# A fused convolution and feed-forward kernel: array halves by token stream, two-bank evictions, quarter-array convolution, a new prologue

## The chip, the core and the metric

The kernel runs on one core of a Trainium2 chip. The core has TensorE (PE, with its weight loads PEld), VectorE (DVE), ScalarE (ACT), GpSimd (POOL) and SyncE (SP), each with its own queue of instructions that it works through in order, and 16 DMA engines that serve transfers issued from those queues. The metric is the device time of one execution in microseconds (us), as the median of several runs. A profiled execution gives, besides its own time, a span: from the first to the last instruction of the program.

## The reference

Input x has 8 sequences of 3904 tokens, 192 features each: 31232 tokens. A causal convolution with 7 taps comes first; the 192 features are 8 heads of 24, and each head has its own softmaxed taps. Then two products with a multiplication between them.

```python
w = softmax(weight)                        # 8 heads x 7 taps
out[b, s, head] = sum_k w[head, k] * x_pad[b, s + k, head]   # 6 zeros ahead of each sequence
x = out.reshape(B * S, D)                  # 31232 x 192
a = x @ w1                                 # 192 -> 1024
b = x @ w2                                 # 192 -> 1024
h = a * b @ w3                             # 1024 -> 1024
return h @ w_out                           # 1024 -> 192
```

Both kernels use that (a * b) @ w3 @ w_out = (a * b) @ (w3 @ w_out): the 1024 x 192 product W is made once on the chip.

## The kernel before

**Convolution.** Tokens go in 32 blocks of 976: 8 windows of 122 tokens, each window loaded with its 6 tokens of history as 128 partitions (`load_x`, L78). POOL casts a block to bf16 (`cast_x`, L185). One head is one matmul with a banded 128x122 matrix `Aband` over 8 windows x 24 features = 192 columns (L199); two heads share a PSUM tile and ACT evicts it to `convo` (L203). POOL then copies feature groups so that a token's row has 384 entries, with every group of 64 features on both sides of a 128-wide piece (L207 to L210).

**Transposing.** For blocks 0 and 1 the layout change is done on PE (`transp`, L228 to L236). From block 2 on, the rows are stored to DRAM (L214) and three DMA transposes per block, more where the ring wraps, write `xT0`, `xT1`, `xT2` (L254), rings of 4096 tokens with features on partitions.

**First product.** `first_product(c)` handles a chunk of 512 tokens. For each of 8 groups of 128 hidden features, a needs three matmuls of 64 rows and so does b: a uses partitions 0 to 63 of the array and b 64 to 127, so a pair runs side by side (L290). `pa` and `pb` are one PSUM bank each out of eight. ACT copies `pa` to bf16 `asb` (L295) and DVE multiplies it by `pb` into `abT` (L296).

**Second product.** `second_product(c, half)` makes 256 tokens x 192 outputs from 16 matmuls with the tokens as weights (L309), ACT copies them out (L312) and SP stores a chunk (L314).

**W.** w3 is loaded in 8 pieces of 128 rows, cast (half on POOL, half on ACT, L327), transposed on PE (L333), evicted by DVE (L336) and multiplied by w_out (L342). This stands after the first products of chunks 0, 1 and 2.

**Order.** The order is written out by hand: the program order of each engine is the order of the calls. After the prologue the loop takes two chunks at a time: two first products, then convolution blocks as far as needed, in between the second products of the chunks three behind. SP issues loads of x, row stores, DMA transposes and output stores in program order and waits where one of them isn't ready. POOL clears the 6 history rows of a window that begins a sequence after the block's load has landed (L83).

Of the kernel before, what the change touches and what calls it, by code (L numbers as in the profile page):

```python
# [17 lines left out]
def kernel(  # L18
# [19 lines left out]
    ST = 122  # L38
    NW = 8
    BLK = ST * NW  # L40
    NB = B * S // BLK
    BPS = S // BLK
    CH = 512
    NCH = B * S // CH
    RING = 8 * CH
    LAG = 3
    PAIR = 2
# [4 lines left out]
    psum = ctx.enter_context(tc.tile_pool(name="psum", bufs=8, space=bass.MemoryType.PSUM))  # L52
    dram = ctx.enter_context(tc.tile_pool(name="dram", bufs=3, space=bass.MemoryType.DRAM))
    ctx.enter_context(tc.manual_schedule())

    def bank(shape, dtype, name):
        return psum.tile(shape, dtype, tag="bank", name=name)

    x_rows = x.rearrange("b s d -> (b s) d")
    o_rows = out  # L60


    wsb = const.tile([128, H, K], FP32)
    nc.scalar.dma_start(out=wsb, in_=weight.partition_broadcast(128))

    def load_x(it):
        xr = work.tile([128, NW, D], FP32, tag="xr", bufs=4, name="xr")
        t0 = it * BLK
        if it == 0:
            nc.gpsimd.memset(xr[0:32, 0, :], 0.0)  # L70
            nc.sync.dma_start(out=xr[PAD:PAD + 112, 0, :], in_=x_rows[0:112, :])
            nc.sync.dma_start(out=xr[PAD + 112:128, 0, :], in_=x_rows[112:ST, :])
            nc.sync.dma_start(
                out=xr[:, 1:NW, :],
                in_=bass.AP(tensor=x.tensor, offset=(ST - PAD) * D,
                            ap=[[D, 128], [ST * D, NW - 1], [1, D]]))
        else:
            nc.sync.dma_start(  # L78
                out=xr,
                in_=bass.AP(tensor=x.tensor, offset=(t0 - PAD) * D,  # L80
                            ap=[[D, 128], [ST * D, NW], [1, D]]))
            if it % BPS == 0:
                nc.gpsimd.memset(xr[0:PAD, 0, :], 0.0)  # L83
        return xr

    xr_of = {0: load_x(0)}

    HC = DFF // 2  # L90
    wf = [stage.tile([128, DFF], FP32, tag=f"w{k}f", bufs=1, name=f"w{k}f") for k in range(3)]
    W_ROWS = ((0, 64), (64, 0), (128, 128))

    def load_w(half):
        cs = slice(half * HC, (half + 1) * HC)
        for k, (r1, r2) in enumerate(W_ROWS):
            nc.sync.dma_start(out=wf[k][0:64, cs], in_=moe_w1[r1:r1 + 64, cs])
            nc.scalar.dma_start(out=wf[k][64:128, cs], in_=moe_w2[r2:r2 + 64, cs])

    load_w(0)  # L100
    xr_of[1] = load_x(1)
    load_w(1)
    xr_of[2] = load_x(2)

    w3r = moe_w3.rearrange("(jt jp) g -> jp jt g", jp=128)
    wo_f = stage.tile([128, JT, D], FP32, tag="wof", bufs=1, name="wo_f")
    nc.sync.dma_start(out=wo_f, in_=moe_w_out.rearrange("(gt gp) d -> gp gt d", gp=128))
    w3f = []
    for jt in range(JT):
        f = stage.tile([128, DFF], FP32, tag="w3f", bufs=JT, name="w3f")  # L110
        nc.sync.dma_start(out=f, in_=w3r[:, jt, :])
        w3f.append(f)


    ident = const.tile([128, 128], BF16)
    make_identity(nc, ident)
    ones = const.tile([128, 1], BF16)
    nc.gpsimd.memset(ones, 1.0)
    dmask = const.tile([128, K, ST], BF16)
    nc.gpsimd.affine_select(  # L120
        out=dmask, in_=ones.unsqueeze(2).to_broadcast([128, K, ST]),
        pattern=[[-1, K], [-1, ST]], compare_op=ALU.is_equal,
        fill=0.0, base=0, channel_multiplier=1)
    Aband = const.tile([128, H, ST], BF16)
    nc.gpsimd.memset(Aband, 0.0)

    CW = 32 + PAD
    QC = [(0, PAD, 32), (32 - PAD, 0, CW), (64 - PAD, 0, CW), (96 - PAD, 0, ST - 96 + PAD)]
    cmask = const.tile([128, K, CW], BF16)
    nc.vector.memset(cmask, 0.0)  # L130
    for q, (c0, j0, n) in enumerate(QC):
        qs = slice(32 * q, 32 * q + 32)
        nc.vector.tensor_copy(out=cmask[qs, :, j0:j0 + n], in_=dmask[qs, :, c0:c0 + n])

    wmax = const.tile([128, H], FP32)
    nc.vector.reduce_max(out=wmax, in_=wsb, axis=AX.X)
    nc.vector.tensor_tensor(
        out=wsb, in0=wsb, in1=wmax.unsqueeze(2).to_broadcast([128, H, K]),
        op=ALU.subtract)
    nc.scalar.activation(out=wsb, in_=wsb, func=ACT.Exp)  # L140
    wsum = const.tile([128, H], FP32)
    nc.vector.reduce_sum(out=wsum, in_=wsb, axis=AX.X)
    nc.vector.reciprocal(out=wsum, in_=wsum)
    nc.vector.tensor_tensor(
        out=wsb, in0=wsb, in1=wsum.unsqueeze(2).to_broadcast([128, H, K]),
        op=ALU.mult)

    HH = H // 2
    cprod = const.tile([128, H, CW, K], FP32)
    cband = const.tile([128, H, CW], BF16)  # L150

    def bands(half):
        hs = slice(half * HH, (half + 1) * HH)
        nc.vector.tensor_tensor(
            out=cprod[:, hs].rearrange("p h j k -> p h k j"),
            in0=cmask.unsqueeze(1).to_broadcast([128, HH, K, CW]),
            in1=wsb[:, hs, :].unsqueeze(3).to_broadcast([128, HH, K, CW]),
            op=ALU.mult)
        with nc.allow_low_precision(reason="one tap and zeros"):
            nc.vector.reduce_sum(out=cband[:, hs, :], in_=cprod[:, hs], axis=AX.X)  # L160
        for q, (c0, j0, n) in enumerate(QC):
            qs = slice(32 * q, 32 * q + 32)
            dst, src = Aband[qs, hs, c0:c0 + n], cband[qs, hs, j0:j0 + n]
            if q % 2 == 0:
                nc.gpsimd.tensor_copy(out=dst, in_=src)
            else:
                nc.scalar.copy(out=dst, in_=src)  # L167


    xT0 = const.tile([128, RING], BF16)  # L170
    xT1 = const.tile([128, RING], BF16)
    xT2 = const.tile([128, RING], BF16)
    xT = (xT0, xT1, xT2)

    PE_BLOCKS = 2
    C = 2 * D

    def cast_x(it, first=False):
        xb = work.tile([128, NW, D], BF16, tag="xb", bufs=2, name="xb")
        xr = xr_of.pop(it)  # L180
        if first:
            nc.scalar.copy(out=xb[:, 0:NW // 2, :], in_=xr[:, 0:NW // 2, :])
            nc.gpsimd.tensor_copy(out=xb[:, NW // 2:NW, :], in_=xr[:, NW // 2:NW, :])  # L183
        else:
            nc.gpsimd.tensor_copy(out=xb, in_=xr)  # L185
        return xb

    convo_of = {}
    rows_of = {}
    xb_of = {}  # L190

    def conv_pair(it, t):
        if t == 0:
            convo_of[it] = work.tile([128, NW, C], BF16, tag="convo", bufs=2, name="convo")
        convo, xb = convo_of[it], xb_of[it]
        cps = bank([128, 2, NW, G], FP32, "cps")
        for r in range(2):
            h = 2 * t + r
            nc.tensor.matmul(  # L199
                cps[0:ST, r], Aband[:, h, :], xb[:, :, h * G:(h + 1) * G],  # L200
                start=True, stop=True)
        dst = convo[0:ST, :, 2 * t * G:(2 * t + 2) * G]
        nc.scalar.copy(  # L203
            out=dst.rearrange("s b (r g) -> s r b g", r=2), in_=cps[0:ST])
        if t == 3:
            del xb_of[it]
            nc.gpsimd.tensor_copy(out=convo[0:ST, :, D:D + 64], in_=convo[0:ST, :, 128:192])  # L207
            if it >= PE_BLOCKS:
                nc.gpsimd.tensor_copy(out=convo[0:ST, :, 256:320], in_=convo[0:ST, :, 64:128])  # L209
                nc.gpsimd.tensor_copy(out=convo[0:ST, :, 320:384], in_=convo[0:ST, :, 0:64])  # L210
                rows = dram.tile([NW, ST, C], BF16, tag="rows", bufs=3, name="rows")
                rows_of[it] = rows
                for a, b in ((0, 112), (112, ST)):
                    nc.sync.dma_start(out=rows[:, a:b, :].rearrange("w s c -> s w c"),  # L214
                                      in_=convo[a:b])
                del convo_of[it]

    def ring_spans(t0, n):
        a = t0 % RING
        if a + n <= RING:  # L220
            return [(0, a, n)]
        return [(0, a, RING - a), (RING - a, 0, n - (RING - a))]

    def transp(it, k):
        convo = convo_of[it]
        tps = bank([128, BLK], BF16, "tps")
        for w in range(NW):
            nc.tensor.transpose(  # L228
                out=tps[:, w * ST:(w + 1) * ST],
                in_=convo[0:ST, w, 128 * k:128 * (k + 1)],  # L230
                identity=ident[0:ST, 0:ST])
# [5 lines left out]
        if k == 1:  # L237
            del convo_of[it]


    def band_products(it):
        for t in range(4):
            conv_pair(it, t)
# [184 lines left out]
```

## Time and profile before

The median of three runs is 560.46 us (559.26 to 560.56).

| | value |
|---|---|
| profiled execution, its own time | 559.08 us |
| its span | 557.3 us |
| mean granted TensorE clock | 0.997 |
| first matmul of the first product | 19.64 us |
| first product of the loop (chunk 3) | 61.9 us |
| DMA moved | 101.60 MB, 182 GB/s mean |
| x loads, row stores, output stores | 768 B pieces |

Read it from the top: the engine shares say which engine is busy; the chain of waits says whose work ended last at each moment; the groups of instructions by line give the duration of one instruction and what its engine waited for. A matmul's recorded duration includes the pipeline, so the pace of matmuls is read from their starts, not from their durations.

### The profile page before, as it was taken

The numbers are of one execution on the slowest core, as the hardware profiler recorded it, in microseconds if no ns is written. First come the engines' busy times: TensorE is split into PE (matmuls) and PEld (weight loads), VectorE is DVE, ScalarE is ACT, GpSimd is POOL, SyncE is SP. The second block draws the span as 40 slices with busy tenths as digits, with TensorE's granted clock in tenths as the row PEclk, the third lists the DMA queues.
The fourth block names the chain that finished last, engine by engine and source line by source line (L and its number), as shares of the span: only waits on it lengthen the run. The fifth ranks groups of instructions, "written<-read, shape, count | busy, mean of one in ns | idle before, by whom it ended". The sixth has DMA issues, their size and how long they took to land.

```text
span 557.3 us, 13715 instructions
## 1 busy us (share of the span) xinstructions
PE 526.0 (94%) x5296; PEld 336.5 (60%) x5296; DVE 335.8 (60%) x516; ACT 405.9 (73%) x761; POOL 112.6 (20%) x154
## 2 busy tenths in 40 slices
PE   0868989999999999999999998999999999999997
PEld 0445666556666556666655666556666556666656
DVE  6446736765556775555776554765556775556770
ACT  2557667877777877777887777877777877776772
POOL 3445030312222112222102222212222112210000
PEclk9989999999999999999999999999999999999999
DMA  7979339997977769767788787998778893665114
GB/s 177 349 258 244 60 87 218 223 247 196 204 181 177 190 166 221 204 175 173 174 223 204 152 202 167 254 221 214 201 180 176 197 222 81 162 143 148 47 33 142
DMA packets 190321, 101.60 MB, mean 182 GB/s; under 512 B 94166, under 2 KB 188464, under 8 KB 190256
## 3 DMA queue, kind: packets, MB, share of 16 engines
q1 hardware_dynamic: 189632, 99.91, 73.3%
q10 hardware_dynamic: 624, 0.82, 0.6%
q8 instruction: 41, 0.67, 0.5%
q14 instruction: 24, 0.20, 0.1%
HBM read 31.74 MB, written 46.47 MB: 140 GB/s over the span
## 4 chain that ended last, share of the span: by engine, by line
PE 82%; issue 2%; POOL 1%; ACT 0%
PE pa L290 50%; PE ops L309 27%; PE cps L199 4%; PE pb L290 1%; POOL xb L185 1%; POOL convo L210 0%; POOL convo L209 0%; ACT osb L312 0%; POOL convo L207 0%
## 5 line engine op out<-in xcount | busy, mean ns | idle before, releaser
L296 DVE TENSOR_TENSOR abT<-asb,pb 128x512 bf16<-128x512 bf16 x488 | 317.0, 688 | 186.1 <-PE pb L290 180.5
L290 PE MATMUL pa<-xT,wb 64*128 64x512 bf16 x1464 | 325.5, 378 | 1.8 <-ACT convo L203 0.7
L290 PE MATMUL pb<-xT,wb 64*128 64x512 bf16 x1464 | 325.3, 378 | 0.6 <-DVE xT L236 0.3
L295 ACT CAST asb<-pa 128x512 bf16<-128x512 f32 x488 | 285.6, 587 | 41.6 <-PE pb L290 14.1
L290 PEld LDWEIGHTS <-wb 64*128 64x128 bf16 x2928 | 141.7, 94 | 176.8 <-issue 13.6
L309 PE MATMUL ops<-W_sb,abT 128*128 128x192 bf16 x1952 | 166.3, 246 | 0.0
L309 PEld LDWEIGHTS <-abT 128*128 128x128 bf16 x1952 | 161.3, 98 | 1.7 <-issue 1.7
L312 ACT COPY osb<-ops 128x384 f32<-128x384 f32 x122 | 58.4, 479 | 79.7 <-PE ops L309 79.2
L207 POOL COPY convo<-convo 122x512 bf16<-122x512 bf16 x32 | 19.7, 615 | 317.3 <-issue 256.9
L203 ACT CAST convo<-cps 122x384 bf16<-122x384 f32 x128 | 52.2, 501 | 6.5 <-PE cps L199 6.5
L199 PE MATMUL cps<-xb,Aband 128*122 128x192 bf16 x256 | 29.1, 258 | 22.2 <-POOL xb L183 14.7
L185 POOL CAST xb<-xr 128x1536 bf16<-128x1536 f32 x31 | 45.5, 1469 | 0.0
L199 PEld LDWEIGHTS <-Aband 128*122 128x122 bf16 x256 | 23.1, 138 | 34.1 <-issue 20.1
L210 POOL COPY convo<-convo 122x512 bf16<-122x512 bf16 x30 | 18.5, 616 | 0.0
L209 POOL COPY convo<-convo 122x512 bf16<-122x512 bf16 x30 | 18.5, 616 | 0.0
L83 POOL MEMSET xr<- 6x192 f32 x7 | 1.7, 249 | 53.6 <-DMA xr<-in_x_dram 53.6
L233 DVE COPY xT<-tps 128x976 bf16<-128x976 bf16 x4 | 2.7, 667 | 9.4 <-PE tps L228 9.3
L342 PE MATMUL wps<-wo_b,w3T 128*128 128x192 bf16 x64 | 6.6, 246 | 1.3 <-DVE w3T L336 1.1
L336 DVE COPY w3T<-w3ps 128x1024 bf16<-128x1024 bf16 x8 | 5.4, 689 | 2.9 <-PE w3ps L333 2.9
L344 ACT CAST W_sb<-wps 128x192 bf16<-128x192 f32 x8 | 2.6, 320 | 6.3 <-PE wps L342 6.3
L342 PEld LDWEIGHTS <-w3T 128*128 128x128 bf16 x64 | 5.1, 98 | 1.7 <-DVE w3T L336 1.7
L167 ACT COPY Aband<-cband 32x152 bf16<-32x152 bf16 (+1 forms) x4 | 1.2, 305 | 6.0 <-DVE cband L160 5.9
(38 smaller groups left out, 50.9 us busy)
## 6 DMA issues: line engine op xcount, KB each, us to landing
xr<-in_x_dram SPq DMA_DIRECT2D x31, 768.0 KB
out_dram<-osb SPq DMA_DIRECT2D x61, 384.0 KB
rows<-convo SPq DMA_DIRECT2D x30, 672.0 KB
w3f<-in_moe_w_dram SPq DMA_DIRECT2D x8, 512.0 KB
rows<-convo SPq DMA_DIRECT2D x30, 60.0 KB
xT<-rows SPq DMA_TRANSPOSE x111
wo_f<-in_moe_w_out_dram SPq DMA_DIRECT2D x1, 768.0 KB
xr<-in_x_dram SPq DMA_DIRECT2D x1, 672.0 KB
```

Of the source, the lines that this page charges most:

```text
L185: nc.gpsimd.tensor_copy(out=xb, in_=xr)
L199: nc.tensor.matmul(cps[0:ST, r], Aband[:, h, :], xb[:, :, h * G:(h + 1) * G], start=True, stop=True)
L203: nc.scalar.copy(out=dst.rearrange("s b (r g) -> s r b g", r=2), in_=cps[0:ST])
L207: nc.gpsimd.tensor_copy(out=convo[0:ST, :, D:D + 64], in_=convo[0:ST, :, 128:192])
L209: nc.gpsimd.tensor_copy(out=convo[0:ST, :, 256:320], in_=convo[0:ST, :, 64:128])
L210: nc.gpsimd.tensor_copy(out=convo[0:ST, :, 320:384], in_=convo[0:ST, :, 0:64])
L290: nc.tensor.matmul(dst, wb[k][rows, ft * 128:(ft + 1) * 128], xT[k][rows, r0:r0 + CH], start=(k == 0), stop=(k == 2))
L295: nc.scalar.copy(out=asb, in_=pa)
L296: nc.vector.tensor_tensor(out=ab[:, ft, :], in0=asb, in1=pb, op=ALU.mult)
L309: nc.tensor.matmul(ops[:, r, :], ab[:, jt, g * 128:(g + 1) * 128], W_sb[:, jt, :], start=(jt == 0), stop=(jt == JT - 1))
L312: nc.scalar.copy(out=osb[:, 2 * half:2 * half + 2, :], in_=ops)
L342: nc.tensor.matmul(wps, w3T[:, gt, :], wo_b[:, gt, :], start=(gt == 0), stop=(gt == JT - 1))
```

## The change

Tokens are split in two streams of 15616: the first four sequences and the last four. Partitions 0 to 63 of the array now hold 64 features of a token of stream 0 and partitions 64 to 127 the same 64 features of stream 1. A round R covers 512 tokens of each stream. `pa` is a for both streams in two PSUM banks (one tile of [128, 2, 512]), `pb` the same for b, so the eight banks are four tiles. ACT and DVE take both banks in one instruction of 1024 elements; `ops` holds 512 tokens of one stream, evicted with 768 elements.

The convolution works on windows of 58 tokens (64 partitions with history). A head is four matmuls: input rows of stream 0 or 1, output columns for the first or second half of the block's windows. Each is a 64x64 matrix. The eviction reads two banks. A token pair's row has 384 entries with no copies, so one row serves both streams; rows go to one DRAM tensor, and a round's three DMA transposes each take 512 rows. Blocks have 10, 10, 10, 26, 24 and then 32 windows of each stream. Weights are kept in two layouts, straight (`wn`) and with halves swapped (`wsw`).

In the prologue 14 matmuls on zeros come first, the Exp table is asked for early, and the convolution of blocks 1 to 3, their stores and transposes stand between the steps of the first products of rounds 0 to 2. All w3 casts are on POOL. The load of block 4 stands between the first product of round 2 and the w3 products; the second product of round 0 follows W.

```diff
-    ST = 122
-    NW = 8
-    RING = 8 * CH
-    LAG = 3
-    PAIR = 2
+    NS = 2
+    TS = B * S // NS
+    NR = -(-TS // CH)
+    RING = 4 * CH
+    LAG = 2
+    Q = 64
+    ST = Q - PAD
+    SIZES = [10, 10, 10, 26, 24] + [32] * 6
...
-    psum = ctx.enter_context(tc.tile_pool(name="psum", bufs=8, space=bass.MemoryType.PSUM))
+    psum = ctx.enter_context(tc.tile_pool(name="psum", bufs=4, space=bass.MemoryType.PSUM))
+    def banks(name):
+        return psum.tile([128, NS, CH], FP32, tag="banks", name=name)
...
+    def load_x(b):
+        for i0, n in halves_of(b):
+            xr = work.tile([128, n, D], FP32, tag="xr", bufs=2, name="xr")
...
+                    for r in range(NS):
+                        q = nc.scalar if b == 0 and r == 1 else nc.sync
+                        q.dma_start(
+                            out=xr[Q * r:Q * r + Q, w:w + m, :],
+                            in_=bass.AP(tensor=x.tensor, offset=(r * TS + tok(i) - PAD) * D,
+                                        ap=[[D, Q], [ST * D, m], [1, D]]))
+                if i % WB == 0:
+                    for r in range(NS):
+                        nc.gpsimd.memset(xr[Q * r:Q * r + PAD, w, :], 0.0)
...
+    def warm(n):
+        t = banks("warm")
+        for j in range(n):
+            nc.tensor.matmul(t[:, j % 2, :], zeros[:, 0:128], zeros, start=True, stop=True)
+
+    warm(14)
...
+    def conv(b, h0, nh, split=False):
...
+        for j in range(nh):
+            h = h0 + j
+            for c in range(2):
+                xb, w0 = xb_of[b][c]
+                for r in range(NS):
+                    nc.tensor.matmul(
+                        view(slice(Q * c, Q * c + Q), r)[:, :, j * G:(j + 1) * G],
+                        Aband[Q * r:Q * r + Q, h, :],
+                        xb[Q * r:Q * r + Q, w0:w0 + n, h * G:(h + 1) * G],
+                        start=True, stop=True)
...
+        for e, (k, c0, m) in enumerate(segments(h0 * G, wd)):
+            dst = convo[:, :, k, :, c0:c0 + m].rearrange("p w r g -> p r w g")
+            f = nc.vector.tensor_copy if split and e % 2 == 1 else nc.scalar.copy
+            f(out=dst, in_=src[:, :, :, o:o + m])
...
+    def transposes(R, first=0):
+        t0, t1 = max(R * CH, first), min((R + 1) * CH, TS)
+        a = t0 % RING
+        for k in range(NP):
+            nc.sync.dma_start_transpose(
+                out=xT[k][:, a:a + t1 - t0], in_=rows[t0:t1, k * 128:(k + 1) * 128])
...
+            for i in range(2):
+                p = banks("pa" if i == 0 else "pb")
+                for k in range(NP):
+                    for r in range(NS):
+                        rs = slice(Q * r, Q * r + Q)
+                        nc.tensor.matmul(
+                            p[:, r, 0:N], w_of(i, k, r)[rs, ft * 128:(ft + 1) * 128],
+                            xT[k][rs, r0:r0 + N],
+                            start=(k == 0), stop=(k == NP - 1))
+            pa, pb = pq
+            asb = work.tile([128, NS, CH], BF16, tag="asb", bufs=3, name="asb")
+            nc.scalar.copy(out=asb[:, :, 0:N], in_=pa[:, :, 0:N])
+            nc.vector.tensor_tensor(out=ab[:, ft, :, 0:N], in0=asb[:, :, 0:N],
+                                    in1=pb[:, :, 0:N], op=ALU.mult)
+            if between and ft in between:
+                between[ft]()
...
-        (nc.gpsimd.tensor_copy if jt % 2 == 0 else nc.scalar.copy)(out=w3b_of[jt], in_=w3f[jt])
+        nc.gpsimd.tensor_copy(out=w3b_of[jt], in_=w3f[jt])
...
+    first_product(0, {
+        4: seq((conv, 1, 0, 4)),
+        5: seq((conv, 1, 4, 4), (cast_x, 3)),
+        6: seq((pe_transposes, 1), (store, 1, 19)),
+        7: seq((conv, 2, 0, 4))})
+    first_product(1, {
+        0: seq((conv, 2, 4, 4), (store, 2), (transposes, 2, 1152)),
+        7: seq((conv, 3, 0, 1), (conv, 3, 1, 1))})
+    for jt in range(4):
+        w3_cast(jt)
+    first_product(2, {
+        1: seq((conv, 3, 2, 1), (conv, 3, 3, 1)),
+        3: seq((conv, 3, 4, 1), (conv, 3, 5, 1)),
+        5: seq((conv, 3, 6, 1), (conv, 3, 7, 1), (store, 3), (transposes, 3), (transposes, 4))})
+
+    xr_of[4] = load_x(4)
     w3_transpose(0)
     for jt in range(JT):
         if jt + 4 < JT:
             w3_cast(jt + 4)
         if jt + 1 < JT:
             w3_transpose(jt + 1)
         w3_product(jt)
+    cast_x(4)
+    for r in range(NS):
+        second_product(0, r)
...
+    for R in range(3, NR + LAG):
+        if R < NR:
+            first_product(R)
+        n = max([-(-(needed(a) - done[0]) // (a - R + 1)) for a in range(R, NR)] + [0])
+        for _ in range(min(n, 2)):
+            conv_head()
+        if R - LAG > 0:
+            for r in range(NS):
+                second_product(R - LAG, r)
+        for _ in range(n - 2):
+            conv_head()
+        if R + 2 < NR:
+            transposes(R + 2)
```

`conv_head` convolves one head of the current block; with a block's first head it loads the next block, with the last it stores the rows and casts the next block. In program order SP's queue thus has, at the end of the prologue: the stores of block 3, the six transposes of rounds 3 and 4, the four loads of block 4. POOL's queue has: casts 0 to 3 of w3, the two clearings in block 4 (a sequence begins at its window 68, in the second half of the block), casts 4 to 7 of w3, the casts of block 4.

## The prediction

> **What bounds the kernel now.** First the engine shares, then the chain of waits in order of time. The chain names whose work ended last, so what a stage is worth is read there.
>
> ```profile
> PE 526.0 (94%) x5296; PEld 336.5 (60%) x5296; DVE 335.8 (60%) x516; ACT 405.9 (73%) x761; POOL 112.6 (20%) x154
> ```
> ```profile
> 296.44 0.32 PE pa L290
> 306.91 0.80 PE cps L199 x8
> 307.71 5.28 PE ops L309 x64
> 312.99 0.32 PE pa L290
> ```
>
> From 81 us on one period of two chunks takes 16.55 us (296.44 to 312.99) and all of it is PE: first product, one convolution block, second product. Matmul starts give the pace:
>
> ```profile
> 302.00 0.38 PE L290 MATMUL pa<-xT,wb 64*128 64x512 bf16 x1
> ...
> 304.15 0.38 PE L290 MATMUL pa<-xT,wb 64*128 64x512 bf16 x1
> ```
>
> Ten pairs in 2.15 us; 96 pairs make 48 x 0.2155 = 10.34 us for two chunks counted as one round of 1024 tokens (a chunk is 24 pairs). The convolution takes 0.80, the second product 64 x 0.0825 = 5.28; 16.55 - 16.42 = 0.13 is left for changing the array's use. ACT and DVE are beside it:
>
> ```profile
> L296 DVE TENSOR_TENSOR abT<-asb,pb 128x512 bf16<-128x512 bf16 x488 | 317.0, 688 | 186.1 <-PE pb L290 180.5
> L295 ACT CAST asb<-pa 128x512 bf16<-128x512 f32 x488 | 285.6, 587 | 41.6 <-PE pb L290 14.1
> L312 ACT COPY osb<-ops 128x384 f32<-128x384 f32 x122 | 58.4, 479 | 79.7 <-PE ops L309 79.2
> L344 ACT CAST W_sb<-wps 128x192 bf16<-128x192 f32 x8 | 2.6, 320 | 6.3 <-PE wps L342 6.3
> ```
>
> So fewer, larger evictions save nothing by themselves: they remove work that hides behind PE. What counts is PE's work, PE's new waits, and the prologue, where the first loop product starts at 61.9.
>
> **Loop, evictions.** ACT rows of 192 and 512 columns (320, 587) give 0.834 ns per column and 0.16 us fixed: 1024 columns cost 1.01 us, 768 cost 0.80. DVE likewise: 0.155 + 1024 x 1.04 ns = 1.22 (the 1.04 from 688 at 512, the 0.155 from what is left). A step of PE is now 6 pairs, 1.293 us, so both keep up. But four tiles replace eight banks. `pb` of step i+2 waits for DVE of step i: `pa` ready 0.84 after the step starts (third pair at 0.43, and ACT started 0.41 after the last pair's start at 280.27), ACT to 1.86, DVE to 3.11, and PE wants the tile at 2.59 + 0.65 = 3.23. It fits by 0.12, less some 0.05 for the signal. At no cost I take it; if two-bank rows cost 0.2 more, each step loses 0.04 (the chain closes every third step), 244 steps 10 us. Where the cover is gone: the second convolution head after a product needs the tile of the last-but-one DVE step, 0.15 late, in 22 rounds: 3.3. Rounds 3 to 6 issue two heads behind the second products, 7 to 10 one: their ACT evictions (0.64 to 0.96 each) then stand ahead of the next `asb`, and `pa` and `pb` come late: 0.6, 0.8, 1.1, 1.1 and four times 0.55: 5.8. Together 9.1.
>
> **Loop, convolution.** 56 heads of four matmuls of 16 x 24 = 384 columns (0.16 each). Four at once: 0.16 a head; all in turn: 0.64; row halves side by side as the pa/pb pairs are, column halves in turn: 0.32. No row shows column halves. The old head took 0.1 for 192 columns although `ops` takes 0.0825 for as many, so weight loads weigh too (L199's loads last 138 ns, L309's 98). I take 0.27, near the row-pair figure: 15.1, with 9 and 36 as bounds. Before, 28 blocks in the loop cost 22.4.
>
> [...]
>
> **Loop, sum.** 27.5 rounds of first product x 10.34 = 284.4; second products of 29.5 rounds x 5.28 = 155.8; heads 15.1; changes of use 28 x 0.13 = 3.6; waits 9.1; end 3.9 (last ops to the span's end: 557.3 - 553.4). 471.9 us. The old loop ran from 61.9 to 557.3 for 58 chunks of the first and 61 of the second product; less 3 x 5.17 and 2 x 2.64 for equal work, 474.6. The loop is a wash.
>
> **Edits at nothing.** DMA falls (rows 24 MB to 12, transposes to half, x loads up 5% with 64 rows for 58 tokens instead of 128 for 122); PE never waited for it in the loop. It could now: block 4 is finished at the end of round 4 behind ACT's last eviction, 2.4 after the second products, then SP issues outputs and five stores (2.2), 1.9 MB land in 8, three transposes take 3.8 and 2 to land: 15.5 to 18, and round 6 comes after 18. The work of round 5 hides it; with a slower store each us is PE's, twice (blocks 4 and 5, before later blocks have the second products as cover too). POOL's casts (two of 3072 columns, 2.9 each by 1469 for 1536) hide behind 3.6 rounds; the swapped weight copies (DVE 0.4, ACT and POOL 0.6 each by L352's rows) behind the conv of block 0 and, for the second halves, four steps of round 0. Gone is the wait for POOL's three copies per block, already hidden but for 2.8 and 3.3 us in two periods (329.5 to 348.9 is one of 19.4); those are in the 474.6.
>
> **Prologue, up to round 2.** Convolution, stores and transposes that moved between product steps fill the 28.8 to 38.5 us in which PE, waiting for POOL's cast, ACT and DVE, did 3 us of work. The band matrices end earlier (no table load of 1.28 on the path, 896 columns instead of 1064), but conv, bands and conv stand in turn on DVE: I put the first product at 18.7 (19.64 before, its second step slow in coming). Round 0: 10.34 + 2 at low clock (before, pairs started 0.43 apart from 21.8 to 26.0) + 3.5 inserted = to 34.5; round 1 to 46.8. Round 2 needs DMA transposes, which in SP's queue stand behind x (4 blocks, 5.5 MB), weights 1.57, w_out 0.79 and w3 4.19: 12.06 MB. Before, 7.3 MB were through at 27.9 us (177 and 349 GB/s in the first two slices), and then
>
> ```profile
> 25.00:30.00 5.00, 4.63 (x38) 2.36 (x35) 3.82 (x7) 4.06 (x8) 0.00 (x0) 1.00 1.03 410
> 30.00:35.00 5.00, 1.89 (x15) 1.88 (x15) 0.15 (x1) 2.29 (x7) 2.03 (x2) 0.79 1.06 357
> 40.00:45.00 5.00, 5.00 (x48) 2.68 (x46) 4.76 (x8) 4.69 (x9) 4.12 (x4) 1.00 0.93 245
> ```
>
> (columns: busy of PE, PEld, DVE, ACT, POOL, clock, DMA share, GB/s). 4.7 MB more at 370 make 41 us, stores 43, three transposes of 1.25 issue 47: round 2 starts at 48. ACT has its 8 x 1.01 and eight heads' evictions of 0.68 there; PE waits 2 for tiles: 14 us, to 62; block 3's last eviction ends at 60.2.
>
> The 14 zero matmuls cost nothing, DMA covers them. [...]
>
> **Prologue, the new wait.** Casts 4 to 7 of w3 (all casts now on POOL) stand behind two clearings of block 4's history rows, and a clearing waits for its load. The old kernel shows such waits, up to 15.4 us long; there nothing that PE soon needed stood behind them:
>
> ```profile
> POOL xr L83 <- DMA xr<-in_x_dram: 53.6, 7, 15.4
> ...
> SPq L254 <- DMA rows<-convo: 77.5, 40, 4.3
> ```
>
> That load stands on SP behind block 3's stores and six transposes:
>
> ```profile
> 77.74 0.86 SPq L214 DMA_DIRECT2D rows<-convo  x2
> ...
> 82.63 7.69 SPq L254 DMA_TRANSPOSE xT<-rows  x6
> ```
>
> Stores to first transpose 4.9 us for 0.73 MB; 1.2 MB here: 6 (4.9 to 6.8). Six transposes 7.7 (6.7 to 9). Loads of 2.36 MB at 245 to 357 GB/s: 6.6 to 9.6, I take 8, and 1 to land. Clearings 2 x 0.25, cast 1.04. From 60.2: 84.4. PE does four transposes and three products of W from 62 (1.1 each pair before, 54.17 to 55.28), reaches the fifth transpose at 66.6 and stands still 18 us (13 to 22); behind it in PE's queue are the rest of W, second product 0 and all of the loop. Then 4 x 1.1, 2.5 at low clock (0.79 in the row above, after a shorter idling), 1.5 for the last product, 5.28: the loop starts at 98.
>
> **Sum.** 98.1 + 471.9 = 570 us of span, against 557.3: the loop gains 2.7, the prologue loses 15.4 against 82.7 for equal work. The profiled execution took 1.8 more than its span, the median of the runs 1.4 more than that execution: 573.
>
> **Rivals.** *The clearing does not hold PE* (load lands by 67, or half so late). For it: POOL idled for 257 us before L207, so small delays hide. Against it: the queue order on SP leaves no way past the transposes. 570 - 18 - 2 = 550 of span; with quarters at 0.16 a head, 544. 553, or 547. This is the faster side. *Quarters run in turn* besides the wait: 56 x (0.64 - 0.27) = 21: 594. For it: no row shows column halves side by side; against: row halves do it perfectly. It decides above 0.55 a head. *The tile wait closes in every step*: +10, 583, if the two-bank rows cost 0.2 more than the line through the ACT and DVE rows.
>
> **How the numbers follow.** Forecast, 0.62: 573, its own range 562 to 583 (stall 13 to 22, heads, start of round 2). Clearing covered 0.17; quarters in turn 0.11; tile wait 0.10. The range to hold 8 in 10 takes in half of the first rival and the third: 552 to 588. No change is within 0.3%, 1.7 us. Faster is the first rival, 0.17; same 0.05 from the forecast's edge; slower 0.78.
>
> **What would show it.** The first cast behind the clearings starts near 83 and PE is idle from about 67 to 84, `w3ps` released by POOL, POOL by the DMA of x; round 2 starts at 48 released by a DMA; rounds from 11 on last 16.4; a head's four matmuls start within 0.3 us; ACT rows 1.01, DVE 1.22. It is wrong if PE's gap in W is under 8 us, or if rounds last under 16 or over 17.

## The result and the profile after

The changed kernel takes 603.64 us (median of four runs, 602.91 to 604.32) against 559.86 us: a ratio of 1.0782 (95% interval 1.0757 to 1.0806), slower by 44 us. The profiled execution took 604.32 us with a span of 602.6. The prediction had 573 us and 570 us of span, so the direction was right and 32.6 us are missing.

First the shares of the engines and the costliest groups, from the page of the kernel after (line, engine, operation, tiles and shapes, count, then busy time, mean ns of one, idle time before and what ended it):

```profile
PE 537.1 (89%) x5452; PEld 342.4 (57%) x5452; DVE 315.9 (52%) x281; ACT 354.2 (59%) x424; POOL 65.6 (11%) x55
...
L360 DVE TENSOR_TENSOR abT<-asb,pb 128x1024 bf16<-128x1024 bf16 (+1 forms) x248 | 297.3, 1204 | 225.6 <-ACT asb L359 189.1
L359 ACT CAST asb<-pa 128x1024 bf16<-128x1024 f32 (+1 forms) x248 | 247.2, 1001 | 75.5 <-PE pa L353 75.0
...
L376 ACT COPY osb<-ops 128x768 f32<-128x768 f32 (+1 forms) x62 | 48.9, 789 | 113.1 <-PE ops L371 111.4
```

ACT fell from 761 to 424 instructions and from 405.9 to 354.2 us, POOL from 112.6 to 65.6, DVE from 335.8 to 315.9. The evictions became cheaper, as the change says. PE went from 94% of its span to 89%: it waits more. For what, the waits of the kernel after say (engine and line waited, what for, us in total, times, longest):

```profile
POOL xr L110 <- DMA xr<-in_x_dram: 132.9, 6, 48.2
PE w3ps L410 <- POOL w3b L404: 21.5, 1, 21.5
PE cps L258 <- ACT xb L134: 12.0, 1, 12.0
PE pa L353 <- DMA xT<-rows: 11.9, 5, 7.0
PE cps L258 <- DVE abT L360: 1.2, 6, 0.3
```

One wait of 21.5 us in W, one of 12.0 before the first convolution, 11.9 for DMA transposes. Together they are 45.4 us, but that this is near the loss is chance: the kernel before also waited at its first convolution, which began at 14.7 us there and at 19.2 here:

```profile
PE cps L199 <- POOL xb L183: 14.7, 1, 14.7
```

The chain of waits of the kernel after shows them in their places (start, duration, what):

```profile
3.02 14.99 DMA xr<-in_x_dram
...
60.52 2.49 DMA xT<-rows
...
76.12 0.32 SPq L294
...
76.49 4.65 DMA rows<-convo
...
91.97 11.38 DMA xr<-in_x_dram
...
103.78 1.05 POOL w3b L404
...
104.87 1.03 PE w3ps L410 x8
...
112.49 5.28 PE ops L371 x64
117.77 0.75 PE pa L353 x6
...
252.73 4.76 PE ops L371 x57
257.49 7.77 DMA xT<-rows
```

Read downwards: block 0's second stream lands at 18.0 us; round 2 stands behind transposes that land at 63.0; the POOL cast behind the clearings starts at 103.8, so PE's fifth transpose of w3 starts at 104.9; the loop starts at 117.8; and deep in the loop the chain stands 7.8 us on the transposes of a round (PE itself waits 7.0 of them). The prediction put this last one at nothing. SP's queue in the stretch before it, in the kernel after:

```profile
243.66 1.59 SPq L379 DMA_DIRECT2D out_dram<-osb  x2
245.34 12.04 SPq L104 DMA_DIRECT2D xr<-in_x_dram  x6
257.49 5.01 SPq L316 DMA_TRANSPOSE xT<-rows  x2
```

Six loads of the next block of x take 12.0 us to issue (three of them 2.6 to 3.2 us each, where each load of block 1 in the prologue took 0.6), and the round's transposes stand behind them.

| | predicted | measured |
|---|---|---|
| first product starts | 18.7 | 29.1 |
| round 2 can run | 48 | 63.1 |
| block 3's last eviction ends | 60.2 | 76.1 |
| POOL's cast behind the clearings ends | 84.4 | 104.8 |
| loop starts | 98 | 117.8 |
| loop | 471.9 | 484.8 |

"Loop" runs from the loop's start to the end of the span. The miss is 19.8 us of prologue and 12.9 of loop.

### The profile page after: what moved, and what is told of

Its sections match the earlier page's. It is cut to its first block, busy times and chain, and to the rows that moved or that the text cites. A ratio compares the mean times of both kernels' runs of the same rounds, so it can differ in the third digit from the quotient of the medians.

```text
span 602.6 us, 12764 instructions
## 1 busy us (share of the span) xinstructions
PE 537.1 (89%) x5452; PEld 342.4 (57%) x5452; DVE 315.9 (52%) x281; ACT 354.2 (59%) x424; POOL 65.6 (11%) x55
## 4 chain that ended last, share of the span: by engine, by line
PE 72%; DVE 8%; ACT 8%; DMA 8%; SPq 2%; issue 2%; POOL 0%; ACTq 0%; POOLq 0%
PE ops L371 27%; PE pa L353 22%; PE pb L353 20%; DVE abT L360 7%; ACT asb L359 6%; DMA xr<-in_x_dram 4%; DMA xT<-rows 2%; PE cps L258 2%; SPq L316 2%; ACT convo L268 2%; DMA rows<-convo 1%; PE wps L419 1%; PE w3ps L410 0%; ACT osb L376 0%; SPq L104 0%
## 5 line engine op out<-in xcount | busy, mean ns | idle before, releaser
L360 DVE TENSOR_TENSOR abT<-asb,pb 128x1024 bf16<-128x1024 bf16 (+1 forms) x248 | 297.3, 1204 | 225.6 <-ACT asb L359 189.1
L359 ACT CAST asb<-pa 128x1024 bf16<-128x1024 f32 (+1 forms) x248 | 247.2, 1001 | 75.5 <-PE pa L353 75.0
L353 PE MATMUL pa<-xT,wn 64*128 64x512 bf16 (+1 forms) x744 | 202.7, 378 | 13.6 <-DMA xT<-rows 11.0
L353 PE MATMUL pb<-xT,wn 64*128 64x512 bf16 (+1 forms) x744 | 203.0, 377 | 2.3 <-DVE abT L360 2.1
L353 PE MATMUL pa<-xT,ws 64*128 64x512 bf16 (+1 forms) x744 | 202.9, 379 | 1.0 <-DMA xT<-rows 0.9
L353 PE MATMUL pb<-xT,ws 64*128 64x512 bf16 (+1 forms) x744 | 199.2, 378 | 0.0
L353 PEld LDWEIGHTS <-wn 64*128 64x128 bf16 x1488 | 138.4, 95 | 98.2 <-issue 17.4
L353 PEld LDWEIGHTS <-ws 64*128 64x128 bf16 x1488 | 131.0, 95 | 80.9 <-issue 14.4
L376 ACT COPY osb<-ops 128x768 f32<-128x768 f32 (+1 forms) x62 | 48.9, 789 | 113.1 <-PE ops L371 111.4
L268 ACT CAST convo<-cps 128x768 bf16<-128x768 f32 (+10 forms) x90 | 52.3, 641 | 2.3 <-PE cps L258 2.3
L410 PE MATMUL w3ps<-ident,w3b 128*128 128x128 bf16 x64 | 5.7, 243 | 21.5 <-POOL w3b L404 21.5
L410 PEld LDWEIGHTS <-w3b 128*128 128x128 bf16 x64 | 4.8, 111 | 22.2 <-POOL w3b L404 21.8
```

The costliest lines, as they stand in the source:

```text
L268: f(out=dst, in_=src[:, :, :, o:o + m])
L353: nc.tensor.matmul(p[:, r, 0:N], w_of(i, k, r)[rs, ft * 128:(ft + 1) * 128], xT[k][rs, r0:r0 + N], start=(k == 0), stop=(k == NP - 1))
L359: nc.scalar.copy(out=asb[:, :, 0:N], in_=pa[:, :, 0:N])
L360: nc.vector.tensor_tensor(out=ab[:, ft, :, 0:N], in0=asb[:, :, 0:N], in1=pb[:, :, 0:N], op=ALU.mult)
L376: nc.scalar.copy(out=osb.rearrange("p (a g) d -> p a (g d)", g=2), in_=ops[:, 0:ng // 2, 0:2 * D])
L410: nc.tensor.transpose(out=tps[:, gt, :], in_=w3b[:, gt * 128:(gt + 1) * 128], identity=ident)
```

## The experiments

**The clearing.** Block 4's two clearings of history rows were put behind all eight w3 casts on POOL; its load stays where it was.

```diff
-    xr_of[4] = load_x(4)
+    xr_of[4] = load_x(4, hold=True)     # keeps the two clearings in `held`
...
         w3_product(jt)
+    for part in held:
+        nc.gpsimd.memset(part, 0.0)
     cast_x(4)
```

> The changed kernel, with block 4's two clearings placed behind the eight w3 casts in POOL's queue instead of between casts 3 and 4; loads, stores and transposes keep their places. Theory (the clearing's wait for the load held PE for 21.5 us): PE's wait for the fifth w3 transpose is gone, W is ready some 21 us earlier; block 4's cast still ends only at about 108, so the first convolution head of round 3 waits some 5 us; time 603.6 - 21 + 5 - 2 (clock) = 583 to 587. Rival (PE would have waited for block 4's load anyway, in the convolution): the 21 us reappear before the first head of round 3, time 598 to 604.

Measured: 584.74 us, ratio to before 1.0443 (1.0404 to 1.0483), 18.9 us less than the changed kernel. Waits of this run:

```profile
POOL xr L485 <- DMA xr<-in_x_dram: 20.0, 2, 17.6
...
PE cps L264 <- POOL xb L140: 3.9, 2, 2.1
```

POOL still waits for the load, but only block 4's own cast is behind it. PE's wait in W is gone, and 3.9 us of it come back at the first convolution of block 4, whose cast ends late. The time is in the theory's range, far from the rival's. The prediction's mechanism is shown: the stall came from two small clearings in an in-order queue.

**Block 0 on one queue.** The second stream's part of block 0 went from ACT's queue to SP's, ahead of the weights.

```diff
-                for r, q in ((0, nc.sync), (1, nc.scalar)):
+                for r, q in ((0, nc.sync), (1, nc.sync)):
...
-                        q = nc.scalar if b == 0 and r == 1 else nc.sync
+                        q = nc.sync
```

> The changed kernel, with the second stream's part of block 0 issued by SP ahead of the weights instead of by ACT beside them. Theory (that part waits its turn behind weight pieces of the other queue): it lands near 12 us instead of 18, the first product starts near 24 instead of 29, time 597 to 599. Rival (loads into 64 partitions are slow on any queue): it lands at 16 to 18, time 602 to 605.

Measured: 600.03 us, ratio 1.0716 (1.0662 to 1.0771), 3.6 less: between the two ranges. The first product's first result comes 7.3 us earlier (first `abT` at 25.2 instead of 32.5), but round 2's only 3.3 (61.8 instead of 65.0). Chain of this run:

```profile
22.51 1.10 PE pa L353 x4
...
37.06 12.61 DMA w3f<-in_moe_w_dram
49.68 4.80 DMA rows<-convo
```

Round 2's transposes stand behind w3's loads, done at 49.7, and behind block 2's stores.

**w3 behind the transposes.** w3's eight loads went behind block 2's stores and round 2's transposes in SP's queue, alone.

```diff
-    for jt in range(2):
-        load_w3(jt)
...
-    for jt in range(2, JT):
-        load_w3(jt)
...
-        0: seq((conv, 2, 4, 4), (store, 2), (transposes, 2, 1152)),
+        0: seq((conv, 2, 4, 4), (store, 2), (transposes, 2, 1152),
+               *((load_w3, jt) for jt in range(JT))),
```

> This run has the changed kernel with one edit: w3's eight loads (524 KB each, 4.19 MB in all; the run before called it 2.36 MB, which is block 4's size) stand behind round 2's three transposes in SP's queue instead of ahead of block 2's stores. In the changed kernel these transposes landed at 63.0 us, and the chain of a run like it shows 12.6 us of w3's loads ahead of the stores. Theory: round 2's first product waits for nothing but these transposes, so everything from it on comes 10 to 13 us earlier, and w3, which is wanted only 15 us later, is still in time for its first four casts; time 591 to 595 us. Rival: w3 now competes with block 3's stores and block 4's load, the clearing that holds POOL comes as late as before, and the gain is lost there; 600 to 605 us.

Measured: 596.82 us, ratio 1.0661 (1.0641 to 1.0681), 6.8 less: between the two. Round 2's first `abT` comes 5.2 us earlier (59.9), not 10 to 13, because the last `abT` of round 1 itself ends only at 58.9: behind the wait for the transposes stood PE's own late start. The wait in W is as before, so nothing was lost there:

```profile
PE w3ps L410 <- POOL w3b L404: 21.6, 1, 21.6
```

The late first product and the late transposes thus hide each other: 3.3 and 5.2 us alone, but 12.3 where both are mended (see the run with all edits, where round 2's first `abT` is at 52.7). The runs in which nothing ahead of round 2 differs from the changed kernel, or only the zero matmuls, have it from 64.3 to 65.7, so each of these figures is good to about a microsecond.

**The loop's loads.** Each load of a block of x goes behind the round's transposes in program order, and so in SP's queue.

```diff
-            xr_of[b + 1] = load_x(b + 1)
+            due.append(b + 1)
...
             transposes(R + 2)
+        while due:
+            b = due.pop()
+            xr_of[b] = load_x(b)
```

> The changed kernel, with the loop's loads of x issued behind the round's transposes instead of ahead of the output stores. Theory (round 11 waits for transposes that stand behind 3.1 MB of x at 220 GB/s): the wait of 9 us at 257 to 266 is gone, and 1 us at 220: time 593 to 595. Rival (the stores of the rows set the transposes, not the load): 602 to 605.

Measured: 593.72 us, ratio 1.0604 (1.0565 to 1.0642), 9.9 less. The wait of PE for transposes in this run, 11.9 before:

```profile
PE pa L353 <- DMA xT<-rows: 4.7, 3, 3.3
```

The theory holds. The round of 26.0 us, from one second product's start to the next, is gone; it is 17.2 now.

**The rate into 64 partitions.** The kernel before, with each load of 128 partitions split into two of 64.

```diff
-            nc.sync.dma_start(
-                out=xr,
...
+            for r in range(2):
+                nc.sync.dma_start(
+                    out=xr[64 * r:64 * r + 64],
```

> The kernel before, with every load of an x block split in two of 64 partitions. Theory (a load into 64 partitions moves 220 GB/s where one into 128 moves 330): in 32 to 36 us, where only x is loaded, the rate falls from 331 to about 220 GB/s, and the prologue is 2 to 6 us longer: 562 to 566. Rival (the rate of the changed kernel comes from its block size and the number of transfers in flight, not from 64 partitions): the rate stays above 300, time 559 to 561.

Measured: 559.96 us, ratio 1.0006 (0.9993 to 1.0018). Stretches while x loads move, first of the kernel before, then of this run (stretch, its length, busy of PE, PEld, DVE, ACT, POOL with counts, clock, DMA share, GB/s):

```profile
32.00:36.00 4.00, 2.89 (x24) 2.80 (x23) 0.60 (x1) 1.63 (x4) 1.05 (x1) 0.61 1.11 331
```

```profile
36.00:40.00 4.00, 2.75 (x20) 1.12 (x22) 1.92 (x3) 2.03 (x3) 0.00 (x0) 1.00 1.14 206
```

The same block of x, the DMA engines' share as high (1.11 and 1.14), 331 against 206 GB/s. The rate theory holds. The 2 to 6 us that it expected are not there: the medians agree. In the profiled execution, the slowest of the eight runs, PE waits 11.0 us for POOL's casts where the kernel before waited 7.6 (the new wait is 3.4 us at 46.7), so a small price may hide in the spread of the runs.

**Both halves at once.** All loads of stream 1 on ACT's queue, those of stream 0 on SP's.

```diff
-                        q = nc.scalar if b == 0 and r == 1 else nc.sync
+                        q = nc.scalar if r == 1 else nc.sync
```

> This run has the changed kernel with all of the second stream's x loads issued on ACT's queue, and the first stream's left on SP's, so that the loads into partitions 0 to 63 and into 64 to 127 can move side by side. In the changed kernel they follow one another on one queue at 215 to 224 GB/s, and one load of block 0 on each queue was the only pair that ran side by side. Theory: 64 partitions at a time is what holds the rate, so two loads side by side move at over 300 GB/s; block 4 (2.36 MB) lands about 3 us earlier and the load issues that stand ahead of round 11's transposes are halved, and the time falls by 5 to 12 us, to 592 to 599 us. Rival: the rate rises, but ACT issues these loads between its evictions, and each issue holds an eviction that TensorE waits for; the time stays at 601 to 606 us. Third possibility: the rate stays under 240 GB/s, since something other than the 64 partitions sets it.

Measured: 599.93 us, ratio 1.0723 (1.0678 to 1.0768), 3.7 less, between the theory's range and the rival's. SP issued two loads into partitions 0 to 63 at 306.57 us, ACT two into 64 to 127 at 307.54. The DMA view of this run from 308 to 328 us, 40 slices of 0.5 us:

```profile
GB/s 26 32 289 323 195 203 209 201 177 206 209 209 184 238 296 354 315 326 343 362 375 369 369 372 373 373 355 204 25 23 158 252 223 220 166 159 0 0 0 0
```

In the trace's packets only SP's first load moves from 310 to 314 us (ACT's, issued at 307.54, move later), at 177 to 209 GB/s, and a packet of 768 B takes 64 to 71 ns. From 315 to 317 us both queues fill a half each, at 296 to 354 GB/s, and a packet takes 39 to 41 ns. The 362 to 375 GB/s behind that are no longer two halves: SP's second load had all but landed by 317.7, and ACT's loads moved beside SP's output stores. From 168.5 to 172 us, in an earlier round, loads into both halves move together for longer, at 316 to 332 GB/s. So in this run a half alone moves at some 205 GB/s (its first microsecond apart, the 289 and 323 of the view, which stays unexplained), and two halves side by side at 296 to 354.

Block 4's loads in the changed kernel, one half at a time, are near the 205: 220 GB/s from 94 to 98 us and 215 from 98 to 102, with 62 and 63 ns as the mean of a packet. In the kernel before, from 32 to 36 us, packets of a load into 128 partitions take 41 ns in the mean, at 331 GB/s. What sets the rate of one half is not shown by any run.

Why the time hardly follows was not taken apart. Two things are seen. The queues often do not start together: for block 4 ACT issued its parts at 78.0 and 87.0 us, SP at 91.5, so they moved in turn. And a load in ACT's queue waits for its buffer like any other and holds the evictions behind it, as the rival had it; in the prologue that is

```profile
ACT asb L359 <- POOL xb L134: 8.0, 1, 8.0
```

which put the first `abT` at 39.9 us instead of 32.5.

**The zero matmuls.** `warm(14)` became `warm(0)`.

> This run has the changed kernel without the 14 matmuls of zeros at its beginning; nothing of the computation is left out. Theory: they cost nothing and bring nothing, since the convolution of block 0 starts at 19.16 us, behind its load and cast, long after them; the time stays within 2 us of the changed kernel's, 601.6 to 605.6 us. Rival: they keep the granted clock up for the first convolution and the first product; without them the clock in the windows from 18 to 32 us is under 0.50, and the time rises by 3 to 8 us, to 606 to 612 us.

Measured: 603.50 us, ratio 1.0775 (1.0749 to 1.0802), as the theory had it. The stretch from 28 us, kernel after and then this run:

```profile
28.00:32.00 4.00, 2.80 (x14) 0.88 (x15) 1.54 (x5) 2.83 (x5) 1.43 (x1) 0.50 1.10 277
```

```profile
28.00:32.00 4.00, 3.35 (x16) 1.20 (x17) 1.03 (x4) 3.31 (x5) 1.99 (x2) 1.00 1.11 274
```

The clock column reads 0.50 with them and 1.00 without, yet six matmuls take 1.28 us in both chains at this point (0.65 from 34.49 us on in the changed kernel's). The rival's sign, a lower clock, is thus not to be read from that column in this stretch; by the pace of the matmuls the first product starts equally slowly in both.

**The order of the heads.** The first stream's second product ahead of the two heads of a round, the second stream's behind them.

```diff
+        second_product(R - LAG, 0)
         for _ in range(min(n, 2)):
             conv_head()
-        if R - LAG > 0:
-            for r in range(NS):
-                second_product(R - LAG, r)
+        second_product(R - LAG, 1)
```

> This run has the changed kernel with one order turned in the loop: the first stream's second product comes ahead of the round's two convolution heads, and the second stream's behind them. In the changed kernel the second head starts 0.49 us after the first (295.028 after 294.545), because it waits for the tile that the multiplication abT of the round's last step still holds. Theory: that wait is on TensorE's path in each of about 22 rounds with two heads, and 0.3 us of it goes each time, so the time falls by 5 to 8 us, to 596 to 599 us. Rival: the wait only changes its place (the second stream's second product then waits for its tile as long), and the time stays at 602 to 605 us.

Measured: 608.68 us, ratio 1.0866 (1.0843 to 1.0889): 5.0 slower, outside both ranges. Most rounds fell from 16.63 to 16.41 us, so the wait for the tile was real and 0.22 of it went. But four rounds took 18.2 to 19.4, and the one of 26.0 grew to 27.8. One of them in this run's chain:

```profile
331.53 0.48 PE cps L258 x8
...
332.52 5.21 DMA xT<-rows
...
337.77 0.39 PE pa L353 x2
```

The heads, and with them the loads of x, now stand behind the first output store in program order, and the transposes behind these loads land 2.5 us later (the last at 35.9 us from the start of the round with the loads, 33.4 in the changed kernel). Two heads take 0.48 us here with no tile wait, 0.24 a head.

**All four edits and the order.** Clearings, block 0, w3's loads and the loop's loads as above, the order of heads, and block 4's load right behind w3's.

> This run has the changed kernel with four edits together: block 4's two clearings behind all eight casts of w3 and its load ahead of nothing that the casts need (19 us alone), both streams of block 0 on SP's queue ahead of the weights (3.6 us alone), the loop's x loads behind the round's transposes (10 us alone), the first stream's second product ahead of the two heads; and a fifth that is new: w3's eight loads stand behind round 2's three transposes in SP's queue instead of ahead of them. Theory: the new edit lets round 2 start some 12 us earlier (its transposes landed at 59.7 us behind w3's 2.36 MB), and half to all of that reaches the loop's start; with the others, 603.6 - 19 - 4 - 10 - 6 - 9 = 556 us, 550 to 562. Rival: w3 now lands late and the eight transposes of w3 wait for it, or the five share their gains; 563 to 575 us.

Measured: 554.22 us (553.16 to 555.16), ratio 0.9897 (0.9875 to 0.9918): 49 us faster than the changed kernel and 1.0% faster than the one before. (The 2.36 MB in the expectation is block 4's size; w3 has 4.19 MB.) The page of this run, shares and chain by line:

```profile
PE 528.9 (96%) x5452; PEld 337.3 (61%) x5452; DVE 315.8 (57%) x281; ACT 353.1 (64%) x424; POOL 66.1 (12%) x55
...
PE ops L377 29%; PE pb L359 26%; PE pa L359 26%; DVE abT L366 3%; ACT asb L365 3%; PE cps L264 2%; ACT convo L274 2%; DMA wf<-in_moe_w_dram 2%; DMA rows<-convo 2%; DMA xr<-in_x_dram 1%; ACT osb L382 1%; DMA xT<-rows 0%; SPq L322 0%; DVE ws L338 0%; PE wps L425 0%
```

PE is back at 96%, and 81% of the chain is the two products.

**The order of heads in the mended kernel.** The same without the turned order.

> This run has the mended kernel with the changed kernel's order of heads (both heads, then both streams' second products). The order alone cost 5 us where the loop's x loads stood ahead of the transposes (608.7 against 603.6), though most rounds fell from 16.63 to 16.40 us; in the mended kernel all rounds from the eleventh on are 16.4. Theory: the order of heads saves 0.23 us in each of some 25 rounds, and lost time only through the x loads, which it issues 2.6 us later and which stand ahead of the transposes in the queue; with the loads behind the transposes only the gain is left, so this run is 4 to 7 us slower than the mended kernel, 558 to 561 us. Rival: the order of heads costs time by itself, and this run is 2 us or more faster, under 552 us.

Measured: 559.29 us, ratio 0.9993 (0.9976 to 1.0010), as the theory had it. The order is worth 5.1 us once the loads stand behind the transposes: it lost before only through them. This is the changed kernel with the four edits and block 4's earlier load, 44.4 us less; singly the four gave 18.9 + 3.6 + 6.8 + 9.9 = 39.2. Two things can make the 5 beyond, and no run parts them: the pair that hid each other, worth 4 us more together at round 2, and block 4's load, which stands this early only here (round 3 takes 19.4 us from its first `abT` to the next round's, with the clearings' edit alone 23.3).

**Two queues in the mended prologue.** Stream 1's loads of blocks 1 to 3 on ACT's queue.

```diff
-                        q = nc.sync
+                        q = nc.scalar if r == 1 and 1 <= b <= 3 else nc.sync
```

> This run has the mended kernel with the second stream's loads of blocks 1, 2 and 3 on ACT's queue (all others on SP's). In the run with two queues the loads into one half of the partitions moved at about 205 GB/s while they were alone, and at 326 to 370 GB/s while one load into each half was under way. The mended kernel's DMA engines are full from 10 to 40 us at 209 to 232 GB/s, and TensorE has some 10 us of idle time there. Theory: blocks 1 to 3 (2.26 MB each 26 windows, less the others) take a third less time where both halves move, and the time falls by 2 to 6 us, to 548 to 552 us. Rival: block 1's second half now runs beside the weights of the first product and delays them, and ACT's waits for the buffers hold its evictions; 554 to 562 us.

Measured: 565.68 us, ratio 1.0110 (1.0070 to 1.0150): 11.5 slower than the mended kernel, so the rival holds, and more strongly than its range. Chains, of the mended kernel and of this run:

```profile
3.27 8.71 DMA wf<-in_moe_w_dram
12.00 8.12 DMA xr<-in_x_dram
```

```profile
3.26 12.22 DMA wf<-in_moe_w_dram
15.49 7.58 DMA xr<-in_x_dram
```

The first product's weights land 3.5 us later: block 1's second half, which is not urgent, now moves beside them. The first `abT` comes 9.6 us later, at 35.1 instead of 25.5. The larger part of that is the other half of the rival, ACT's wait for a buffer. The chain of this run:

```profile
31.58 1.79 POOL xb L140
33.39 0.64 ACTq L106
34.07 1.02 ACT asb L365
```

In ACT's queue a load of block 3 stands ahead of the first eviction of `pa`; its buffer comes free when POOL has cast block 2, at 33.4, and ACT is idle for 6.3 us until its eviction starts at 34.1.

## Why the prediction was wrong, step by step

**Right: the new wait.** Clearings that hold the w3 casts were predicted with their place and the queue behind them, at 18 us (13 to 22). The trace has 21.5 and the run without them gives 18.9 back. Of the way from block 3's last eviction to the cast (24.2 predicted, 28.7 measured) the stores were 1 us shorter, the six transposes 1 longer (8.7), and block 4's loads 4.5 longer: from their first issue at 89.9 to the clearing at 103.5, against 8 + 1.

**Wrong: the loads' rate (a term mis-sized, used twice, and left out in the loop).** The prediction took "Loads of 2.36 MB at 245 to 357 GB/s" and "4.7 MB more at 370" from stretches in which weights and 128-partition loads moved. Loads into 64 partitions, one after the other, moved at some 205 to 220 in these runs. Block 4 took 11.4 us and its issues 2 more instead of 9. The 12.06 MB were to be "through at 41"; in the run with block 0 on one queue they were at 49.7. The rate makes a difference of that size: an estimate from 5.5 MB of x, 25.0 us at 220 against 14.9 at 370, is 10 us. The stores then took 4.8 instead of 2. In the loop six such loads, 3.1 MB in all, hold SP's queue for 12.0 us.

**Wrong: "I put the first product at 18.7".** It started at 29.1. The step counted DVE's work from the convolution on and did not ask when block 0 lands: on two queues, beside the weights, its second half landed at 18.0 and the convolution started at 19.2. On one queue ahead of the weights the first product starts at 21.8 (the chain shows its matmuls from 22.5), still 3 late: there DVE's bands, evictions and copies stand in turn from 14.3 to 21.8, with one gap of 1.2 us. This was worth only 3.6 us by itself, since the transposes stood behind it; with them mended it counts in full (round 2's first `abT` at 52.7 instead of 59.9).

**Wrong: "round 2 starts at 48".** 63.1, from the two steps above: 11.7 with block 0 landing early (59.7), 3.4 more without. The order on SP was seen rightly, its length was not.

**Half right: the loop.** "The loop is a wash" holds for PE's work. With the queues mended and the prediction's own order of heads the loop runs from 82.8 us, when round 3 has its transposes, to 559.4: 476.6, against 471.9 predicted and 474.6 for the kernel before. (The 470.3 of the mended kernel, from 83.1 to 553.4, has the turned order.) Most of the 4.7 over are rounds that were put too short: an estimate is 3 us from thirteen rounds of 16.63 instead of 16.4, and 1.4 from the eight before them, whose waits came to 7.2 where 5.8 was predicted. A head takes 0.24 against 0.27, its four matmuls start within 10 ns (294.541 to 294.551), and the rows of 1024 columns took 1.01 on ACT and 1.22 on DVE, as predicted. The two-bank rows keep up, as the third rival denied, and the quarters run side by side, as the second denied. The tile wait of the second head was put at 0.15 a round and gave 0.22 back. But the margin for the DMA was sought in the wrong place: the prediction asked whether a block's stores and transposes fit into 18 us, and not which loads of x stand ahead of the transposes in the same queue. That cost 9.9 us.

**The first rival** (the clearing does not hold PE) did not come true. That its time, 553 us, is near the 554.2 of the mended kernel is chance: that kernel has the turned order of heads, worth 5.1 us, and w3, block 0 and block 4 in other places, and its loop starts at 83 where the rival's sum has it at 78.

Not tried: a load that fills both halves of the partitions from one queue in small alternating pieces, which might keep the rate at 331 GB/s without a second queue.

## What to carry to other kernels

When a change splits a transfer, look at the bytes and at which partitions each piece fills: two transfers into 64 partitions each, one after the other, moved at 206 GB/s where one into 128 moved at 331. For every in-order queue write down what each wait now has behind it, DMA issues too: two clearings of 0.25 us cost 18.9 us, loads that nothing was waiting for cost 9.9, and in ACT's queue a load that waited for its buffer held the evictions for 6.3. Two late things on one path hide each other, so edits judged one at a time can look small (3.3 and 5.2 us at round 2) and give more together (12.3).

## What the runs showed that was not expected

In the run with two queues a DMA packet of 768 B took 64 to 71 ns while one half of the partitions was being filled and 39 to 41 ns while both were. All four 64x64 matmuls of a head start within 10 ns in the changed kernel (294.541 to 294.551 us), and so do their weight loads (294.540 to 294.550). In the run without zero matmuls the clock column reads 1.00 from 28 to 32 us, while six matmuls take 1.28 us, as in the changed kernel, which reads 0.50 there and has 0.65 for six from 34.49 us on.
